# A transformer block on one core: its feed-forward part put in source order on every engine, with fixed places for small operations

## The chip, the cores and the metric

The kernel runs on one core of one Trainium2 chip. The metric is the device time of one execution in microseconds (us). Before the change it is 1748.71 us, the median of three runs (1748.16 to 1749.04). A core has five instruction queues that matter here: PE (TensorE, the matmuls), DVE (VectorE), ACT (ScalarE), POOL (GpSimd), each of which works through its instructions in the order in which they stand, and SP, which here only issues DMA transfers.

## The reference

One block on 2048 rows of width 512, batch 1:

```python
x = A_x
mod = (_silu(c) @ w_mod).reshape(c.shape[0], 6, 1, -1)
sa, ca, ga, sb, cb, gb = (mod[:, 0], mod[:, 1], mod[:, 2], mod[:, 3], mod[:, 4], mod[:, 5])
h = _layernorm(x, axis=-1) * (1 + ca) + sa
x = x + ga * _A_ref(h, A_k_cache, A_v_cache, A_wq, A_wo)
h = _layernorm(x, axis=-1) * (1 + cb) + sb
x = x + gb * _B_ref(h, B_w_gate, B_w_up, B_w_down)
return x
```

`_A_ref` is attention with 32 query heads over a cache of 512 keys; `_B_ref` is `(gelu(x @ w_gate) * (x @ w_up)) @ w_down` with a hidden width of 1792. The change touches the second half, the feed-forward part.

## The kernel before, in words

**Numbers in two halves.** Every matmul operand is held as a pair of float16 tiles, a high part (the value rounded) and a low part (the value less the high part). A product of two such pairs is three matmuls (`mm3`, L86, the matmuls' own line is L90). Making a pair is called parting: a copy to float16 on one engine, then a subtraction.

**The feed-forward part.** The hidden width is 14 slices of 128, taken two at a time: a pair of slices n. The rows are taken in two groups of 1024, so n runs from 0 to 13, and `q` from 0 to 27 (L1742): the even q is the gate set of a pair, the odd q its up set. A set is a 2 x 2 block product made with seven products instead of eight (`product`, L854; `CHAIN`, L865), in the order 1, 2, 6, 7, 5, 4, 3 (`ORDER`, L1610). Each product is 6 matmuls of 128x512. Products 1, 6, 7 and 4 add up in one PSUM bank, `fa`; 2 is in `fb`; 5 and 3 in `fc`. After products 1, 6 and 7 ScalarE copies `fa` out (`keep`, L883, line L885), because the bank goes on adding; so the next product into `fa` waits for that copy. VectorE then adds the other bank to the copy (L1270). For a gate set ScalarE applies gelu (L1276); for an up set VectorE multiplies by the gate (L1287). The four quarters of the result are called 11, 21, 22 and 12; they become ready after products 2, 4, 5 and 3.

**The projection down.** For n = 0 to 4 and 7 to 11 (`turned(n)`) it is again a seven-product block product, transposed, in two rounds of seven groups of 3 matmuls (`yt_tasks`, L1711). It needs the parted quarters 11, 21, 22 and four sums: t1 = 12 - 11, t3 = 22 - 12, t2 = 22 - t1, t4 = 21 - t2 (`sums_of`, L1300). GpSimd makes the sums (L1303) and their low parts; ScalarE makes the high parts (L1297); the low parts are L1298, on VectorE for the plain quarters. After each group VectorE adds the bank, scaled, to an accumulator `yt` (L1664, L1667). For the other four pairs it is a plain product with 8 tiles of rows, 6 matmuls each (`py`), added by VectorE (L952). These groups are slipped in, two at a time, after four of the seven products of the sets that follow (`y_next`).

**Beside it** in the first row group: the second LayerNorm of rows 1024 to 2047 (`ln_turned`, L529: load, normalize on ScalarE L539, part on ScalarE L543 and GpSimd L544, transpose by DMA), its transposed tiles scaled and shifted (`turned_out`, L553: ScalarE L558, VectorE L559, a store), and the block sums of these (`combos`, L562: GpSimd differences L574, parting on ScalarE L374 and GpSimd L378), at fixed steps (a step is one product of a set; step s is q = s // 7, product number s % 7 in the order). At the end of each row group the accumulators are turned back: a regrouping copy on GpSimd (`yt_turn`, L1678, line L1683), a DMA transpose, a copy to rows (L1701) and an addition (L1643).

**What sets the order.** `tick` runs what `put_off(k, ...)` put off by k steps (L456, L460). The attention part is written under a manual schedule for all engines (L1536): the instructions of each queue stand in the order of the source. The feed-forward part stands under a manual schedule for SP alone (L1535): DMAs are issued in source order, and a scheduler, with its own estimates of durations, arranges PE, DVE, ACT and POOL around them.

## Time and profile before

| | |
|---|---|
| median of 3 runs | 1748.71 us |
| the profiled execution's own time | 1750.29 us |
| its span (first to last instruction) | 1748.5 us |
| mean granted TensorE clock | 0.997 |
| matmuls recorded | 8020 |
| feed-forward part, from about | 1330 us on |
| DVE, ACT and POOL busy over the span | 82%, 70%, 62% |

A row of a timeline gives the start in us from the start of the span, the busy time in us, engine, line, operation, tiles written and read, shapes, a count if equal rows were merged, and in square brackets the idle time of the engine before it with what ended it. A row of groups gives the count, the busy time in us, the mean of one in ns, and the idle time ahead. A matmul's recorded time has a tail that overlaps the next one.

### The profile page before, as it was taken

To read this page: it belongs to the slowest core of one execution; us is meant where nothing else is said; L and a number is where in the kernel's file an instruction comes from. 1 tells how busy PE (TensorE), PEld (TensorE's weight loads), DVE (VectorE), ACT (ScalarE), POOL (GpSimd) and SP (SyncE) were. 2 spreads that over 40 slices of the span, in tenths; PEclk is the share of its full clock that TensorE was granted. 3 is DMA by queue.
4 is the path that set the end of the run, shared out by engine and by line. 5 is a ranking of instruction groups with operands and counts; after the bars stand their busy time and mean duration, and the time that the engine had idled before them with its cause. 6 is when DMAs were issued, how large, how long until landed. Compare 5 with 4: busy or idle time off the path is not lost.

```text
span 1748.5 us, 26169 instructions
## 1 busy us (share of the span) xinstructions
PE 1717.0 (98%) x8020; PEld 787.3 (45%) x8022; DVE 1425.4 (82%) x2454; ACT 1228.4 (70%) x2781; POOL 1085.5 (62%) x1298
## 2 busy tenths in 40 slices
PE   8999999999999999999999999999999999999998
PEld 5444444444444444444444444444444444444443
DVE  7898898888889899888887888888886787666665
ACT  5988788888879777888787777788773644333431
POOL 4889778776788884655585675654521648452435
PEclk9999999999999999999999999999999999999999
DMA  6999999999999998999999999999986753643245
GB/s 231 221 198 212 216 214 206 223 205 222 212 220 228 206 208 183 213 212 235 200 217 231 211 208 216 204 225 216 198 178 142 199 170 135 166 139 103 88 125 137
DMA packets 690637, 339.83 MB, mean 194 GB/s; under 512 B 578880, under 2 KB 601408, under 8 KB 690496
## 3 DMA queue, kind: packets, MB, share of 16 engines
q1 hardware_dynamic: 690208, 337.63, 85.6%
q8 instruction: 63, 1.03, 0.2%
q14 instruction: 78, 0.64, 0.1%
q10 hardware_dynamic: 288, 0.52, 0.1%
HBM read 135.66 MB, written 61.87 MB: 113 GB/s over the span
## 4 chain that ended last, share of the span: by engine, by line
PE 84%; DVE 5%; ACT 4%; POOL 3%; DMA 2%; issue 1%; SPq 1%; DVEq 0%; POOLq 0%; ACTq 0%
PE py L90 19%; PE ps L90 17%; PE po L90 17%; PE qa L90 8%; PE fa L90 7%; PE qc L90 4%; PE fc L90 3%; PE ya L90 2%; PE qb L90 2%; PE fb L90 2%; PE yc L90 1%; PE pq L90 1%; ACT ee L991 1%; ACT p L1003 1%; DVE nm L982 1%
## 5 line engine op out<-in xcount | busy, mean ns | idle before, releaser
L991 ACT ACTIVATE ee<-ps,nm 128x512 f32<-128x512 f32 x512 | 349.9, 683 | 194.4 <-DVE nm L982 190.1
L1008 DVE SCALAR_TENSOR_TENSOR p<-ee,rr,p 128x512 f16<-128x512 f32 x512 | 456.7, 892 | 3.9 <-ACT p L1003 3.3
L982 DVE TENSOR_REDUCE nm<-ps 128x1 f32<-128x512 f32 x512 | 350.6, 685 | 110.4 <-PE ps L90 107.5
L90 PE MATMUL ps<-k,qt 128*128 128x512 f16 x1536 | 415.6, 380 | 5.4 <-ACT ee L991 4.2
L1003 ACT ACTIVATE p<-ee,rr 128x512 f16<-128x512 f32 x512 | 364.4, 712 | 19.3 <-DVE rr L999 9.7
L90 PE MATMUL po<-pt,v 128*128 128x512 f16 x1536 | 373.1, 379 | 2.1 <-DMA pt<-p 1.2
L90 PE MATMUL py<-wo,ot 128*128 128x512 f16 x1536 | 371.6, 379 | 0.0
L90 PEld LDWEIGHTS <-w 128*128 128x128 f16 x2184 | 213.6, 98 | 269.1 <-DMA w<-kept 7.1
L90 PEld LDWEIGHTS <-v 128*128 128x128 f16 x1536 | 149.8, 98 | 184.3 <-DMA pt<-p 2.4
L90 PEld LDWEIGHTS <-ot 128*128 128x128 f16 x1536 | 150.1, 98 | 181.9 <-DVE ot L740 0.5
L90 PEld LDWEIGHTS <-qt 128*128 128x128 f16 x1536 | 145.9, 98 | 177.4 <-issue 5.4
L1303 POOL TENSOR_TENSOR fg<-fg 128x512 f32<-128x512 f32 x40 | 52.5, 1314 | 117.2 <-DVE fg L1287 116.5
L740 DVE SCALAR_TENSOR_TENSOR ot<-po,ot 128x512 f16<-128x512 f32 x128 | 87.7, 685 | 36.3 <-ACT ot L739 35.9
L1297 ACT ACTIVATE at<-fg 128x512 f16<-128x512 f32 x86 | 53.2, 626 | 89.4 <-DVE fg L1287 56.5
L991 ACT ACTIVATION_READ_ACCUMULATOR ee<-ps,nm 128x1 f32 x512 | 99.9, 195 | 0.0
L952 DVE SCALAR_TENSOR_TENSOR acc<-py,ysc,acc 128x512 f32<-128x512 f32 x128 | 94.7, 740 | 6.2 <-PE py L90 6.2
L235 POOL TENSOR_TENSOR lw<-lw,half__86 128x1 f32<-128x1 f32 x37 | 22.9, 619 | 104.5 <-DVE lw L185 104.5
L90 PE MATMUL fa<-t,w 128*128 128x512 f16 x336 | 83.0, 379 | 2.3 <-DMA w<-kept 1.4
L90 PE MATMUL qa<-t,w 128*128 128x512 f16 x348 | 84.9, 379 | 0.0
L397 POOL TENSOR_TENSOR rs<-rs,nhalf 128x1 f32<-128x1 f32 x32 | 18.7, 584 | 104.2 <-DVE rs L391 101.3
L739 ACT ACTIVATE ot<-po 128x512 f16<-128x512 f32 x128 | 73.7, 576 | 5.0 <-PE po L90 5.0
L159 POOL TENSOR_TENSOR stage<-rw,stage 128x512 f16<-128x512 f32 (+1 forms) x56 | 64.7, 1155 | 4.7
(241 smaller groups left out, 2796.5 us busy)
## 6 DMA issues: line engine op xcount, KB each, us to landing
w<-kept SPq DMA_DIRECT2D x123, 256.0 KB, 3.5
wo<-kept SPq DMA_DIRECT2D x70, 256.0 KB, 3.5
kept<-stage SPq DMA_DIRECT2D x61, 256.0 KB, 3.3
raw<-in_wo SPq DMA_DIRECT2D x56, 256.0 KB, 3.2
kept<-w SPq DMA_DIRECT2D x39, 256.0 KB, 3.4
rw<-in_wq SPq DMA_DIRECT2D x38, 256.0 KB, 3.2
hs<-hf SPq DMA_DIRECT2D x32, 256.0 KB, 3.2
pt<-p SPq DMA_TRANSPOSE x512, 3.5
```

What stands on the lines that cost most here:

```text
L90: nc.tensor.matmul(ps, a, b, start=first and n == 0, stop=last and n == 2, skip_group_check=chain)
L159: nc.gpsimd.tensor_tensor(dst[:, 1, :], src, dst[:, 0, :], op=ALU.subtract)
L235: nc.gpsimd.tensor_tensor(out, out, half_, op=ALU.pow)
L739: nc.scalar.activation(t[:, 0, :], src, AF.Copy, scale=scale)
L740: return lambda: nc.vector.scalar_tensor_tensor(t[:, 1, :], src, scale, t[:, 0, :], op0=ALU.mult, op1=ALU.subtract)
L952: nc.vector.scalar_tensor_tensor(acc[ti], st["p"], by, acc[ti], op0=ALU.mult, op1=ALU.add)
L982: nc.vector.tensor_reduce(nm, E[t]["ps"], axis=AX.X, op=ALU.max, negate=True)
L991: nc.scalar.activation(e, E[t]["ps"], AF.Exp, bias=E[t]["nm"], scale=1.0, accum_out=sm[:, t % 2:t % 2 + 1])
L1003: nc.scalar.activation(p16[:, 0, :], E[t]["e"], AF.Copy, scale=E[t]["r"])
L1008: nc.vector.scalar_tensor_tensor(p16[:, 1, :], E[t]["e"], E[t]["r"], p16[:, 0, :], op0=ALU.mult, op1=ALU.subtract)
L1297: nc.scalar.activation(t[:, 0, :], g, AF.Copy)
L1303: nc.gpsimd.tensor_tensor(g[o], g[a], g[b], op=ALU.subtract)
```

## The change

Five things change, all in the feed-forward part.

1. The whole of it is put under a manual schedule for all engines: PE, DVE, ACT and POOL now stand in source order, as SP did.
2. The subtraction that makes the low part is put off. For 11, 22 and 12 it comes two steps after the high part. For 21 it comes just before the sum that follows product 3.
3. The four sums are made one after another on GpSimd, and their parting is put off: high parts 2 steps (t1), 3 (t3, t2) and 4 (t4) later, low parts 4 (t1, t2) and 5 (t3, t4) later.
4. The LayerNorm steps get fixed places: loads 5 steps ahead instead of 4, turning 4 steps after instead of 5, other start steps; the VectorE half of `turned_out` is put off by two steps and its store by four; the block sums start 8 steps later.
5. The regrouping copy of `yt_turn` moves from GpSimd to ScalarE.

```diff
-        nc.vector.scalar_tensor_tensor(v, TURN[qb][:, :, KT + dt, :], sc, v, op0=ALU.mult, op1=ALU.add)
-        put_off(3, lambda: dma(spilled(3, qb)[:, dt, :], f))
+        put_off(2, lambda: nc.vector.scalar_tensor_tensor(v, TURN[qb][:, :, KT + dt, :], sc, v, op0=ALU.mult, op1=ALU.add))
+        put_off(4, lambda: dma(spilled(3, qb)[:, dt, :], f))
...
-        def parts(key, g, eng):
+        def high_of(key, g):
             t = A[n, key] = pair("ot", "at", NOT)
             nc.scalar.activation(t[:, 0, :], g, AF.Copy)
+
+        def low_of(key, g, eng):
+            t = A[n, key]
             eng.tensor_tensor(t[:, 1, :], g, t[:, 0, :], op=ALU.subtract)
+
+        def parts(key, g):
+            high_of(key, g)
+            if key == "21":
+                st["low"] = lambda: low_of(key, g, nc.vector)
+            else:
+                put_off(2, lambda: low_of(key, g, nc.vector))
 
         def sums_of():
             g = {k: G.pop((n, k)) for k in ("11", "12", "21", "22")}
             for o, a, b in (("11", "12", "11"), ("12", "22", "12"), ("22", "22", "11"), ("21", "21", "22")):
                 nc.gpsimd.tensor_tensor(g[o], g[a], g[b], op=ALU.subtract)
-                parts({"11": "t1", "12": "t3", "22": "t2", "21": "t4"}[o], g[o], nc.gpsimd)
+            for key, o, high, low in (("t1", "11", 2, 4), ("t3", "12", 3, 5), ("t2", "22", 3, 4), ("t4", "21", 4, 5)):
+                put_off(high, lambda key=key, o=o: high_of(key, g[o]))
+                put_off(low, lambda key=key, o=o: low_of(key, g[o], nc.gpsimd))
...
             elif k == 3:
+                if "low" in st:
+                    st["low"]()
                 add("u2", "c")
                 out_("12", st["u2"])
...
-    for i in range(2 * QT):
-        q = 7 * (2 + i // 2) + 3 * (i % 2)
+    for i, q in enumerate((16, 19, 22, 26, 30, 33, 36, 40)):
         load, norm, split, turn = ln_turned(i)
-        step(q - 4, load)
+        step(q - 5, load)
         step(q, norm)
         step(q + 1, split)
-        step(q + 5, turn)
-    for k, (qb, dt) in enumerate(((0, 0), (0, 2), (0, 1), (0, 3), (1, 0), (1, 2), (1, 1), (1, 3))):
-        step(33 + 2 * k if k < 4 else 41 + k, lambda qb=qb, dt=dt: turned_out(qb, dt))
+        step(q + 4, turn)
+    for q, (qb, dt) in zip((37, 41, 44, 47, 50, 51, 54, 55), ((0, 0), (0, 2), (0, 1), (0, 3), (1, 0), (1, 2), (1, 1), (1, 3))):
+        step(q, lambda qb=qb, dt=dt: turned_out(qb, dt))
     for p in range(2):
-        q = 53 + 14 * p
+        q = 61 + 14 * p
...
-            nc.gpsimd.tensor_copy(u, YT[g, c, qb].bitcast(U16).rearrange("p (r h) -> p h r", h=2))
+            nc.scalar.activation(u, YT[g, c, qb].bitcast(U16).rearrange("p (r h) -> p h r", h=2), AF.Copy)
...
+    ctx.enter_context(tc.manual_schedule())
     f_done = {(0, k) for k in ORDER} | {(1, 1), (1, 2), (1, 6)}
     for q in range(NQ):
```

More of the change, by code (lines that the diff above doesn't have):

```diff
@@ L1288, in result @@
                 if not turned(n):
-                    parts(key, G.pop((n, key)), nc.vector)
+                    parts(key, G.pop((n, key)))
                 elif key != "12":
-                    parts(key, g, nc.vector)
+                    parts(key, g)
                 else:
                     sums_of()
-        def parts(key, g, eng):
+        def high_of(key, g):
             t = A[n, key] = pair("ot", "at", NOT)
             nc.scalar.activation(t[:, 0, :], g, AF.Copy)
+        def low_of(key, g, eng):
+            t = A[n, key]
             eng.tensor_tensor(t[:, 1, :], g, t[:, 0, :], op=ALU.subtract)
+        def parts(key, g):
[4 more added lines that the diff above has]
+                put_off(2, lambda: low_of(key, g, nc.vector))
         def sums_of():
```

## The prediction

> **What bounds the kernel now.** I read the page's first part, then the windows of the feed-forward part, then who PE waits for there.

> ```profile
> span 1748.5 us, 26169 instructions
> ...
> PE 1717.0 (98%) x8020; PEld 787.3 (45%) x8022; DVE 1425.4 (82%) x2454; ACT 1228.4 (70%) x2781; POOL 1085.5 (62%) x1298
> ```
> ```profile
> 1330.00:1540.00 210.00, 202.53 (x934) 90.81 (x933) 145.03 (x205) 92.28 (x152) 119.05 (x112) 1.00 0.54 156
> 1540.00:1700.00 160.00, 160.00 (x743) 72.44 (x742) 107.90 (x155) 61.03 (x99) 59.12 (x48) 1.00 0.38 119
> 1700.00:1748.50 48.50, 40.17 (x176) 17.02 (x173) 27.12 (x36) 8.15 (x13) 26.12 (x21) 0.94 0.53 139
> ```
> ```profile
> PE fa L90 <- DMA w<-kept: 5.3, 3, 2.2
> PE yc L90 <- ACT at L1297: 2.6, 2, 2.0
> PE py L90 <- ACT at L1297: 1.6, 2, 0.8
> PE fc L90 <- DVE fg L1270: 1.0, 1, 1.0
> PE fa L90 <- ACT fg L885: 0.6, 1, 0.6
> PE py L90 <- DVE at L1298: 0.4, 1, 0.4
> PE fa L90 <- ACT fu L885: 0.2, 1, 0.2
> ```

> PE is the bound: 98% of the span, and 160.00 of 160 us in the middle stretch. (The columns are PE, PEld, DVE, ACT, POOL, clock, DMA share, GB/s.) The change adds and removes no matmul, so it can only act through what PE waits for, in 418.5 of 1748.5 us. Those waits are the seven rows (from 1290 us on): 11.7 us in 11 waits. Two things come on top.

> ```profile
> 1484.27 0.59 PE L90 MATMUL yc<-at,wo 128*128 128x512 f16 x2 [1.95 <-ACT at L1297]
> 1484.69 1.46 PE L90 MATMUL fb<-b,w 128*128 128x512 f16 x6
> ...
> 1711.72 1.46 PE L90 MATMUL fc<-b,w 128*128 128x512 f16 x6
> 1715.43 2.46 PE L90 MATMUL fa<-b,w 128*128 128x512 f16 x6 [2.24 <-DMA w<-kept]
> 1717.68 2.20 PE L90 MATMUL fb<-b,w 128*128 128x512 f16 x6
> ```

> Six matmuls normally show 1.46 us; the next start comes 1.30 us after (0.216 each), so a tail of 0.16 us overlaps. Each wait loses that overlap too: 11 x 0.16 = 1.8 us. And after the wait of 2.24 us the next twelve matmuls ran at half rate: 2.46 + 2.20 - 2 x 1.46 = 1.74 us. After the wait of 1.95 us none did. So **15.2 us are lost now** (11.7 + 1.8 + 1.7), the most that the change can win.

> **What it removes.** The order of the built instructions shows that it does what it says: on PE, DVE, ACT and POOL the feed-forward part stands in source order.

> ```profile
> L1683 POOL COPY yu<-yt 128x1024 uint16<-128x1024 uint16 x16 | 17.2, 1098 | 29.0 <-DVE yt L1664 26.5 <-DMA yv<-yu 2.5
> ```
> ```profile
> SPq L1688 <- POOL yu L1683: 29.6, 4, 12.4
> ```

> SP, already in source order, stood 29.6 us behind transposes whose input POOL had not yet copied; weight loads are queued behind them, and PE's 5.3 us of DMA waits follow. With the copy on ACT at its source place I let these waits go, with their clock loss, and what is late next is in the sum below. The two `py` rows are at the very end: there the new order puts two tiles of pair 12 (12 matmuls, 2.6 us) between the last product 3 and the first tile of pair 13, and the low parts it needs are made in that time. I let all 15.2 us go.

> **What it adds: one new chain a pair.** In the new order ACT makes the high parts of t3 and t2 *before* it copies `fa` after product 6 of the next gate set (both put off by 3 steps). Product 7 waits for that copy, and t2 is GpSimd's third subtraction. In the scheduler's order nothing forced that. The durations:

> ```profile
> L1303 POOL TENSOR_TENSOR fg<-fg 128x512 f32<-128x512 f32 x40 | 52.5, 1314 | 117.2 <-DVE fg L1287 116.5
> L1298 POOL TENSOR_TENSOR at<-fg,at 128x512 f16<-128x512 f32 x40 | 48.7, 1226 | 1.1 <-ACT at L1297 1.1
> L1297 ACT ACTIVATE at<-fg 128x512 f16<-128x512 f32 x85 | 52.5, 626 | 87.5 <-DVE fg L1287 54.7 <-POOL fg L1303 32.7
> L574 POOL TENSOR_TENSOR cb<-cb 128x512 f32<-128x512 f32 x8 | 11.5, 1436 | 0.1
> L378 POOL TENSOR_TENSOR t<-cb,t 128x512 f16<-128x512 f32 x8 | 10.1, 1268 | 0.0
> L559 DVE SCALAR_TENSOR_TENSOR hf<-xt,cols,hf 128x512 f32<-128x512 f16 x8 | 9.1, 1181 | 1.8 <-ACT hf L558 1.8
> ```
> ```profile
> 1585.78 0.63 ACT L1297 ACTIVATE at<-fg 128x512 f16<-128x512 f32 x1
> 1586.44 0.69 DVE L1298 TENSOR_TENSOR at<-fg,at 128x512 f16<-128x512 f32 x1 [0.69 <-ACT at L1297]
> 1587.05 0.74 DVE L1287 SCALAR_TENSOR_TENSOR fg<-fg,gsc,fa 128x512 f32<-128x512 f32 x1
> ...
> 1589.02 0.68 DVE L1298 TENSOR_TENSOR at<-fg,at 128x512 f16<-128x512 f32 x1
> 1589.62 0.68 DVE L1270 TENSOR_TENSOR u<-u,fc 128x512 f32<-128x512 f32 x1
> 1590.22 0.75 DVE L1664 SCALAR_TENSOR_TENSOR yt<-yb,dyc,yt 128x512 f32<-128x512 f32 x1
> 1590.88 0.68 DVE L1270 TENSOR_TENSOR fg<-fg,fb 128x512 f32<-128x512 f32 x1
> 1591.48 0.75 DVE L1287 SCALAR_TENSOR_TENSOR fg<-fg,gsc,u 128x512 f32<-128x512 f32 x1
> ...
> 1592.37 2.62 POOL L1303 TENSOR_TENSOR fg<-fg 128x512 f32<-128x512 f32 x2 [15.70 <-DVE fg L1287]
> ...
> 1597.90 0.58 ACT L885 ACTIVATE fg<-fa 128x512 f32<-128x512 f32 x1
> 1598.61 0.60 ACT L885 ACTIVATE u<-fa 128x512 f32<-128x512 f32 x1
> ```

> Queued on DVE, an addition or a low part takes 0.60 us to the next start, a scaled addition or multiplication 0.66 (0.72 if it needs the one just before), and its result is there after 0.75; POOL starts 0.14 after that, two subtractions take 2.62 us, a third 1.27 (0.04 of overlap); a full ACT starts a part each 0.54. Handing over between other engines costs 0.03 to 0.05.

> Take t = 0 where DVE can start the sum after product 5 of an up set. Its queue then is: that sum 0; multiply 22 at 0.72; multiply 21 at 1.37; low part of 22 at 2.18 (its high part on ACT runs 1.51 to 2.14); two `yt` additions 2.78, 3.44; low part of 21 at 4.10; the sum after product 3 at 4.70; multiply 12 at 5.42, done 6.17. POOL subtracts from 6.31, the third is done at 10.16; ACT makes t2's high part from 10.18, copies `fa` 10.72 to 11.32; PE can go at 11.37. PE's own way from t = 0 is 48 matmuls, less the tail and the hand-over: 48 x 0.216 - 0.20 = 10.17. **PE waits 1.2 us.** Product 3's sum alone was ready 0.8 us before its place in the queue.

> Ten pairs have such sums. By the order of each:
> - n = 8 to 11: 4 x 1.2 = 4.8; n = 1 the same, 1.2.
> - n = 0: only 36 matmuls lie between (no groups of an earlier pair), and no `yt` additions: chain 10.1, own way 7.6, 2.5 us.
> - n = 2: one VectorE half of `turned_out` (1.18) stands ahead of the gate's sum, so gelu, which is ahead of t2 on ACT, is a little late: 1.4.
> - n = 3: two such halves stand there; sum after product 2 at 9.8, gelu 10.5, t3, t2 and the copy behind it to 12.7: 2.5.
> - n = 4: 1.2, and POOL's order there puts two block-sum differences and two low parts (2 x 1.44 + 2 x 1.27 = 5.4) between the four subtractions (done 11.4) and the low parts of t1 and t2 (2 x 1.2): t2 is whole at 19.2, PE wants it at 68 x 0.216 + 1.2 = 15.9: 3.3 more.
> - n = 7: beside a plain pair, one addition fewer: 0.6.
> - The 16 regrouping copies on ACT: no row has ACT doing 1024 numbers. It lies between one 512 part (0.63) and two (1.25); I take 1.05, near two, since the size is doubled. Most have cover: ACT was idle 87.5 us before its parts alone. In the gate set of pair 6 three of them and three other parts stand ahead of the copy of `fa`: about 1.0 us; with 0.63 each nothing, with 1.25 some 1.6.

> Together 4.8 + 1.2 + 2.5 + 1.4 + 2.5 + 4.5 + 0.6 + 1.0 = **18.5 us**. Two of these, at n = 0 and n = 4, are longer than the 2.24 us after which the clock halved; 2 x 1.74 = 3.5. The place of n = 3 is near that limit, and I leave it out. The put-off low parts cost PE nothing: 11, 21 and 22 are needed 4 to 15 us after. LayerNorm loads go out a step earlier, stores later; their readers are over 10 us away.

> **The sum:** 18.5 + 3.5 - 15.2 = +6.8 us on the profiled execution's 1750.29 us, 1757.1. That execution is 1.6 us above the median, so I put the median at 1748.71 + 6.8 = **1755.5**.

> [...]

> **The rivals.**
> - *No half rate.* The new waits come, but spread so that no stretch of PE is idle enough; 1.95 us cost nothing in this trace. Then 18.5 - 15.2 = +3.3: 1752.0, just inside no change. [...] For it: mean clock 0.997, only one such stretch.
> - *Faster.* The chain has 1.2 us less than I count, because the waits feed back on each other: any stop of PE inside the 48 matmuls gives DVE, POOL and ACT that time. Point from which it decides: chain 10.2 us or less. Then n = 1, 2, 8 to 11 and 7 cost 0.2 at most, n = 0 and 3 cost 1.3 each, n = 4 3.3, pair 6 1.0, clock 1.7: 8.8 - 15.2 = -6.4: 1742.3. For it: in the middle stretch the same operations made PE wait for nothing.
> - *Weights still late.* If ACT's copies come late in their turn, SP stays behind transposes as now: 5.3 + 0.5 + 1.7 stay: 1763. Against: ACT has more free time there than POOL.
> - That the order doesn't change is excluded by the built program.

> **Chances.** Forecast 0.50; no half rate 0.20; faster 0.18; weights late 0.12. A measurement tells about 0.2% (3.5 us) from no change: slower 0.62, same 0.20, faster 0.18. The forecast's own range is 1752.5 to 1760. The range to hold 8 in 10 takes in no half rate and reaches half into the two outer cases: 1743 to 1763. It covers copies of 0.63 and 1.25 us.

> **What would show it.** Right: in the profile after, PE's largest row is `fa` waiting for ACT L885, about 1 us each, ten times, 27 us apart; the waits for weights are gone; a wait for POOL's low part once, near the tenth set. Wrong: no such row, or rows for weights; a wait of over 2.3 us without half rate refutes the clock term, a POOL subtraction well under 1.2 us the chain.

## The result, and the profile after

The changed kernel takes **1762.76 us** (median of 4 runs, 1761.17 to 1763.47), the kernel before on the same chip 1748.43 us (4 runs, 1747.65 to 1749.04): ratio 1.0081, 95% interval 1.0063 to 1.0098. It is 14.3 us slower. The forecast was 6.8 us slower, 1755.5.

The page's first part, after:

```profile
span 1761.0 us, 26246 instructions
...
PE 1718.3 (98%) x8020; PEld 788.1 (45%) x8022; DVE 1415.7 (80%) x2454; ACT 1242.6 (71%) x2797; POOL 1063.9 (60%) x1282
```

PE's busy time is the same as before to 1.3 us (1717.0), its span is 12.5 us longer: PE waits more. In the middle stretch, where PE was busy for 160.00 of 160 us, it is now busy for 154.38 (columns as in the prediction's table):

```profile
1540.00:1700.00 160.00, 154.38 (x710) 69.33 (x709) 100.86 (x145) 58.46 (x95) 57.31 (x47) 1.00 0.36 112
```

Whom PE waits for from 1290 us on:

```profile
PE fa L90 <- ACT fg L885: 14.7, 14, 3.4
PE ya L90 <- DVE yt L1677: 6.5, 10, 0.7
PE fa L90 <- ACT u L885: 1.0, 1, 1.0
```

The waits for weights and the two at the very end for parts are gone. In their place stand 14 waits for ScalarE's copy of `fa`, and ten, which the forecast did not have, of a group of the projection down for an addition to `yt`. In this kernel's line numbers L885 is the copy, L1297 a high part, L1301 a low part, L1313 a subtraction of the sums, L1677 an addition to `yt`, L1270 a sum of two banks, L1287 a multiplication.

Below, **lost** is what matmul starts are apart beyond 0.216 us, summed from 1330 us on; it takes in the lost overlap and half-rate stretches. Before the change it is 15.3 us, after it 29.5. The difference, 14.2, agrees with the 14.3 us between the medians. The two profiled spans differ by less, 12.5 us, because the profiled execution of the kernel before lost some 2 us more ahead of 1330 us (18.2 against 16.0). By place, beside the forecast:

| place | forecast | lost: `ya` + product 7 + product 4 |
|---|---|---|
| n = 0 | 2.5 | 2.72 (product 7) |
| n = 1 | 1.2 | 0.82 + 0.70 + 0.48 = 2.00 |
| n = 2 | 1.4 | 0.82 + 1.11 + 0.92 = 2.85 |
| n = 3 | 2.5 | 0.82 + 2.07 = 2.89 |
| n = 4 | 4.5 | 0.82 + 1.24 + 3.55 = 5.61 |
| pairs 5 and 6 | 1.0 | 0.82 + 0.33 = 1.15 |
| n = 7 | 0.6 | 0.73 |
| n = 8 to 11 | 4.8 | 4 x (0.82 + 0.77) = 6.4 |
| end | 0 | 0.82 + 1.14 = 1.96 |
| half rate | 3.5 | 3.3 in two stretches |
| sum | 22.0 | 29.6 |

The largest of these places, n = 4, where ScalarE's copy waits for a GpSimd low part and PE for the copy:

```profile
1493.10 0.60 ACT L885 ACTIVATE fg<-fa 128x512 f32<-128x512 f32 x1 [5.02 <-POOL at L1301]
...
1493.75 1.55 PE L90 MATMUL fa<-t,x 128*128 128x512 f16 x6 [3.39 <-ACT fg L885]
```

Pair 9 in the timeline, the rows of its chain:

```profile
1624.55 1.46 PE L90 MATMUL fa<-t,x 128*128 128x512 f16 x6
1624.82 0.69 DVE L1270 TENSOR_TENSOR u<-u,fc 128x512 f32<-128x512 f32 x1 [1.76 <-PE fc L90]
...
1626.99 0.69 DVE L1301 TENSOR_TENSOR at<-fg,at 128x512 f16<-128x512 f32 x1
...
1628.45 0.75 DVE L1677 SCALAR_TENSOR_TENSOR yt<-ya,dyc,yt 128x512 f32<-128x512 f32 x1
...
1629.12 0.68 DVE L1301 TENSOR_TENSOR at<-fg,at 128x512 f16<-128x512 f32 x1
1629.25 0.81 PE L90 MATMUL ya<-at,wo 128*128 128x512 f16 x3 [0.65 <-DVE yt L1677]
...
1631.33 5.33 POOL L1313 TENSOR_TENSOR fg<-fg 128x512 f32<-128x512 f32 x4 [19.00 <-DVE fg L1287]
...
1634.75 1.21 ACT L1297 ACTIVATE at<-fg 128x512 f16<-128x512 f32 x2
...
1635.87 0.58 ACT L885 ACTIVATE fg<-fa 128x512 f32<-128x512 f32 x1
...
1636.50 0.81 PE L90 MATMUL fa<-t,w 128*128 128x512 f16 x3 [0.61 <-ACT fg L885]
```

The forecast chain is there, step by step: from the sum after product 5 to product 7 it takes 1636.50 - 1624.82 = 11.68 us, against 11.37 forecast and 10.17 of PE's own. PE loses this time in two portions: 0.82 at a group of three matmuls, whose bank VectorE empties late because a low part stands ahead of the addition, and 0.77 at product 7.

### The profile page after: what moved, and what is told of

Same layout as the page of the kernel before. It is cut to its first block, busy times and chain, and to the rows that moved or that the text cites. A ratio compares the mean times of both kernels' runs of the same rounds, so it can differ in the third digit from the quotient of the medians.

```text
span 1761.0 us, 26246 instructions
## 1 busy us (share of the span) xinstructions
PE 1718.3 (98%) x8020; PEld 788.1 (45%) x8022; DVE 1415.7 (80%) x2454; ACT 1242.6 (71%) x2797; POOL 1063.9 (60%) x1282
## 4 chain that ended last, share of the span: by engine, by line
PE 83%; DVE 7%; ACT 5%; POOL 2%; issue 2%; DMA 1%; DVEq 0%; SPq 0%; POOLq 0%; ACTq 0%
PE py L90 19%; PE ps L90 17%; PE po L90 17%; PE qa L90 8%; PE fa L90 6%; PE qc L90 4%; PE fc L90 3%; PE ya L90 2%; PE qb L90 2%; PE fb L90 2%; ACT ee L991 1%; PE yc L90 1%; ACT p L1003 1%; PE pq L90 1%; DVE nm L982 1%
## 5 line engine op out<-in xcount | busy, mean ns | idle before, releaser
L90 PE MATMUL ps<-k,qt 128*128 128x512 f16 x1536 | 414.9, 379 | 5.6 <-ACT ee L991 4.5
L90 PE MATMUL po<-pt,v 128*128 128x512 f16 x1536 | 372.9, 379 | 1.8 <-DMA pt<-p 1.8
L90 PE MATMUL py<-wo,ot 128*128 128x512 f16 x1536 | 371.5, 379 | 0.1
L90 PEld LDWEIGHTS <-w 128*128 128x128 f16 x2184 | 213.8, 98 | 272.6 <-issue 16.9
L90 PEld LDWEIGHTS <-v 128*128 128x128 f16 x1536 | 149.9, 98 | 184.1 <-DMA pt<-p 2.0
L90 PEld LDWEIGHTS <-ot 128*128 128x128 f16 x1536 | 150.2, 98 | 181.7 <-DVE ot L740 0.5
L90 PEld LDWEIGHTS <-qt 128*128 128x128 f16 x1536 | 145.9, 98 | 177.0 <-issue 4.5
L1313 POOL TENSOR_TENSOR fg<-fg 128x512 f32<-128x512 f32 x40 | 51.9, 1298 | 151.5 <-DVE fg L1287 149.1
L1297 ACT ACTIVATE at<-fg 128x512 f16<-128x512 f32 x86 | 53.3, 626 | 79.2 <-DVE fg L1287 74.3
L90 PE MATMUL fa<-t,w 128*128 128x512 f16 x336 | 81.6, 379 | 11.2 <-ACT fg L885 10.2
L90 PE MATMUL qa<-t,w 128*128 128x512 f16 x348 | 84.9, 379 | 0.0
L90 PE MATMUL ya<-at,wo 128*128 128x512 f16 x240 | 63.9, 382 | 6.5 <-DVE yt L1677 6.5
```

Of the source, the lines that this page charges most:

```text
L90: nc.tensor.matmul(ps, a, b, start=first and n == 0, stop=last and n == 2, skip_group_check=chain)
L1297: nc.scalar.activation(t[:, 0, :], g, AF.Copy)
L1313: nc.gpsimd.tensor_tensor(g[o], g[a], g[b], op=ALU.subtract)
```

## Experiments

All kernels are edits of the changed kernel unless said otherwise. Each time stands beside the kernel before run on the same chip (medians 1748.1 to 1749.1). In the diffs `...` stands for lines left out, and a line that begins inside a statement is the changed piece of it. All waits and losses are read in the one profiled execution of each kernel, from 1290 or 1330 us on; where that execution lies off the median, the text says so.

### The low part of 22 behind the additions to yt

```diff
-            if key == "21":
-                st["low"] = lambda: low_of(key, g, nc.vector)
+            if key in ("21", "22"):
+                st["low" + key] = lambda: low_of(key, g, nc.vector)
...
+                    st["low22"]()
+                    st["low21"]()
                 add("u2", "c")
```

> The changed kernel with one thing altered: VectorE's low part of 22 stands behind the two additions to yt, still ahead of the low part of 21 and of the sum after product 3, so that GpSimd's start stays as it is in VectorE's queue and no low part runs beside GpSimd. Theory A (one chain a pair): the ten waits of 0.82 us for yt go, but in the eight pairs in which GpSimd's subtractions follow, product 7 then waits that much longer for the copy of fa (0.77 becomes 1.5 to 1.6 us in pairs 8 to 11); only the two places without subtractions behind them win, 1.6 us: 1762.8 - 1.6 = 1761 us. Rival B (the wait for yt is a loss of its own beside the chain): 1762.8 - 8.2 = 1754.6 us.

Measured: 1763.16 us, ratio 1.0083 (1.0069 to 1.0096), the changed kernel's time. PE's waits:

```profile
PE fa L90 <- ACT fg L885: 20.1, 14, 3.9
...
PE ya L90 <- DVE yt L1678: 0.6, 2, 0.4
```

`ya`'s 6.5 us went to 0.6, and the wait for the copy grew from 14.7 to 20.1; in pairs 8 to 11 product 7 loses 1.38 instead of 0.77, and 0.09 is left at `ya`, 1.47 together against 1.59. Theory A holds in the main: in a pair with sums the wait for `yt` is a part of the chain, taken early, and moving it wins next to nothing. The 1.6 us that theory A expected from the two places without sums does not show in the time; in this execution other losses stand against it, among them a wait of 1.0 us for weights.

### Low parts behind the last multiplication

The same two low parts were put further back, right behind the multiplication of 12.

```diff
                 nc.vector.scalar_tensor_tensor(g, g, col("gsc", n % NP), src, op0=ALU.mult, op1=ALU.mult)
+                if key == "12":
+                    st["low21"]()
+                    st["low22"]()
```

> The changed kernel with one thing altered: in the up sets VectorE's low parts of 21 and 22 stand right behind the multiplication of 12 (and ahead of GpSimd's subtractions in the program, which overwrite their input), instead of ahead of the additions to yt and of the sum after product 3. Theory A: the ten waits of 0.82 us for an addition to yt go (8.2 us). The sum after product 3 starts as soon as the product is there, 0.8 us earlier in the chain, so GpSimd starts about 0.8 us earlier against PE's own way, and the wait of product 7 for the copy of fa shrinks from 0.77 to about 0.5 us: 1762.8 - 8.2 - 10 x 0.3 = 1751.6 us. Rival B (what is won at ya is lost again at the copy, since the chain through GpSimd alone sets the pace): ya goes, the wait for the copy grows to about 1.6 us, 1762 us.

Measured: 1768.89 us, ratio 1.0112 (1.0097 to 1.0127): slower than the change. `ya` is free, and product 7 loses 1.63 in pairs 8 to 11: the number of rival B, and more than the shorter queue should leave. Pair 9, VectorE and GpSimd:

```profile
1633.92 2.36 DVE L1304 TENSOR_TENSOR at<-fg,at 128x512 f16<-128x512 f32 x2
...
1634.14 5.96 POOL L1316 TENSOR_TENSOR fg<-fg 128x512 f32<-128x512 f32 x4 [18.48 <-DVE fg L1287]
```

Two low parts take 2.36 us instead of 1.3, and the four subtractions beside them 5.96 instead of 5.33. VectorE is so late for the next gate's sum that gelu, which stands ahead of the copy of `fa`, is late too. The slowdown is taken up below. The profiled execution (1766.12 us, clock 0.998) is the shortest of the four; the other three, 1768.2 to 1769.7, have clocks of 0.995 and 0.996, so part of the 6 us over the change is probably half rate that this trace does not show.

An earlier form put the low parts off by two and four steps, alone and together with the edits of the next two sections.

```diff
-                put_off(2, lambda: low_of(key, g, nc.vector))
+            put_off(4 if key == "22" else 2, lambda: low_of(key, g, nc.vector))
```

There they are made from what GpSimd's subtractions have left in the tiles of 21 and 22, so both kernels compute other low parts than the reference needs, and VectorE has to wait for GpSimd:

> The changed kernel with one thing altered: VectorE's low parts of 21 and 22 in the up sets stand behind the multiplication of 12 and the additions to yt, instead of ahead of them (low part of 21 put off by two steps, of 22 by four). Theory A (the queues in source order): in the changed kernel PE waits 0.82 us ten times for an addition to yt (ya, 8.2 us together) because a low part of 0.60 us and an earlier addition stand ahead of it; this wait goes. The sum after product 3 also comes some 0.8 to 1.2 us earlier, and with it GpSimd's four subtractions; since PE now also arrives 0.82 us earlier, the wait of product 7 for the copy of fa shrinks only a little, from 0.77 to about 0.5 us. 1762.8 - 8.2 - 10 x 0.3 = 1751.6 us. Rival B (one chain: what is won at ya is lost again at the copy of fa, since the chain through GpSimd sets the pair's pace): ya goes, but the wait for the copy grows to about 1.6 us; 1762 us.

> The changed kernel with the three alterations together: low parts of 21 and 22 behind the multiplication of 12, high parts of t3 and t2 behind the copy of fa, block operations five steps later in pair 4. Theory A (four separate queue places account for the whole loss): of the 29.5 us that PE loses from 1330 us on in the changed kernel, 8.2 (ya), 12 (copy of fa), 4.5 (product 4) and 3.3 (half rate) go; 1762.8 - 28 = 1734.8 us, which is 13.6 us less than the kernel before. What is left: the two VectorE halves in pair 3 and about 1 us at the end. Rival B (the waits feed on one chain, and PE meets the next late result a little further on): a sum of the single gains is not reached; about 1748 us, no better than the kernel before.

Measured: 1834.99 and 1831.48 us, ratios 1.0493 (1.0477 to 1.0508) and 1.0473 (1.0457 to 1.0488). They answer neither question; they show what a wait of VectorE for GpSimd costs: in the first, PE waits 24.4 us in ten places for a low part and 47.9 us in twelve for the copy of `fa`, with half rate besides: the granted clock is 0.977 over the span and 0.93 from 1540 to 1700 us.

### High parts behind the copy of fa

```diff
-("t3", "12", 3, 5), ("t2", "22", 3, 4)
+("t3", "12", 4, 5), ("t2", "22", 4, 4)
```

> The changed kernel with one thing altered: ScalarE's high parts of t3 and t2 are put off by four steps instead of three, so they stand behind the copy of fa after product 6, not ahead of it. Theory A: the waits of product 7 for that copy (13.1 us in 12 places, 0.77 us in each of pairs 8 to 11) go nearly all, and with the 2.72 us at the first of them also the 1.7 us of half rate that follow it; the low parts of t2 come in time (18 matmuls, 3.9 us, lie between product 7 and the first group that reads t2). The waits for yt and the 3.55 us of pair 4 stay. 1762.8 - 12.5 - 1.7 = 1748.6 us. Rival B (the wait only moves on): the groups of the next pair then wait for t2's low part about as long as product 7 waited for the copy; about 1759 us.

Measured: 1757.44 us, ratio 1.0049 (1.0033 to 1.0066): 5 us of the expected 14. In pairs 8 to 11 product 7 waits no more, and 0.14 is left at product 4. But in pairs 0, 1, 2 and 4 product 4 now loses 1.45, 1.19, 2.04 and 4.58 (7.1 with the half rate behind it): the *next* copy of `fa` has no buffer, because its tile still holds t1's sum until GpSimd has made t1's low part. Pair 2, ScalarE and GpSimd:

```profile
1430.32 1.61 POOL L544 TENSOR_TENSOR xh<-xs,xh 128x512 f16<-128x512 f32 x1
1431.89 3.38 POOL L1301 TENSOR_TENSOR at<-fg,at 128x512 f16<-128x512 f32 x3
...
1433.07 0.60 ACT L885 ACTIVATE fg<-fa 128x512 f32<-128x512 f32 x1 [2.04 <-POOL at L1301]
```

A LayerNorm parting (L544) stands ahead of that low part. (The profiled execution took 1762.44 us, the other three 1757.0 to 1757.6. It lost 20.9 us ahead of 1330 us, against 16.0 in the change's; from 1330 us on it lost 24.1 against 29.5, which is the 5 us of the medians.) So neither theory is right as it stood: the wait does move on, but to a buffer, not to t2's low part.

### Block operations later in pair 4

```diff
-                step(q + 2 * off, fn)
+                step(q + 2 * off + (5 if p == 0 and off > 3 else 0), fn)
```

> The changed kernel with one thing altered: of the first half of GpSimd's block sums in the feed-forward part, the differences and low parts that stand between the subtractions and the low parts of pair 4 are put five steps later. Theory A: ScalarE's copy of fa after product 7 in pair 4 stood idle 5.02 us for GpSimd's low part of t1, because the copy goes into the buffer that this low part still reads, and four block operations (4.8 us) stand ahead of it. With these gone the wait of 3.55 us at product 4 goes, and with it the half rate of 1.63 us behind it; all other waits stay: 1762.8 - 5.2 = 1757.6 us. Rival B (GpSimd is late there by the subtractions alone, or the displaced block operations are late for another pair): 1761 us or more, with a wait at the same place or one new in pair 5 or 6.

Measured: 1769.33 us, ratio 1.0117 (1.0102 to 1.0132). The wait of 3.55 us in pair 4 is gone, as theory A has it, and a larger one is there 17 us later:

```profile
1510.90 1.46 PE L90 MATMUL fa<-t,w 128*128 128x512 f16 x3 [8.27 <-DMA w<-kept]
```

SP stood 10.57 us at the loads for the second half of the block sums, which wait for buffers that the first half now frees later; the weight load behind them was late. Rival B's second form.

### Which of the edits does what: order, copies, put-off parts

The kernel before with the fixed order alone; the change without the fixed order; the change with the regrouping copy back on GpSimd. The edits, in this order:

```diff
+    ctx.enter_context(tc.manual_schedule())
     f_done = {(0, k) for k in ORDER} | {(1, 1), (1, 2), (1, 6)}
...
-    ctx.enter_context(tc.manual_schedule())
     f_done = {(0, k) for k in ORDER} | {(1, 1), (1, 2), (1, 6)}
...
-            nc.scalar.activation(u, YT[g, c, qb].bitcast(U16).rearrange("p (r h) -> p h r", h=2), AF.Copy)
+            nc.gpsimd.tensor_copy(u, YT[g, c, qb].bitcast(U16).rearrange("p (r h) -> p h r", h=2))
```

> The kernel before with one line added: the fixed source order on PE, VectorE, ScalarE and GpSimd for the feed-forward part; no copy, low part, LayerNorm step or block sum is moved. Theory A (a fixed order makes each engine wait where the program puts a dependent instruction right behind its source): GpSimd makes each low part directly behind its subtraction and waits for ScalarE's high part in between, four times (1.31 + 0.63 + 1.14 each, 12 us instead of 5.3 before the copy of fa can go); product 7 waits some 6 us in ten pairs, each followed by a half-rate stretch of about 1.7 us: 1748 + 10 x 7.7 = about 1825 us. Rival B (the order alone costs no more than with the edits, so the put-off parts do nothing): about 1765 us.

> The changed kernel without its fixed source order on the engines: the scheduler places the feed-forward part again, as in the kernel before, and the other edits (copies on ScalarE, low parts put off, LayerNorm and block places) stay. Theory A (the fixed order makes the loss, the copies on ScalarE win back the waits for weights): the waits for yt and for the copy of fa are gone as before the change, the 5.3 us of waits for weights and their 1.7 us of half rate are gone too; about 1743 us. Rival B (the moved places of the other edits cost by themselves, with the scheduler following them): 1755 us or more. Rival C (the scheduler's order brings back the waits for weights whatever engine copies): 1748 us.

> The changed kernel with one thing undone: the 16 regrouping copies are on GpSimd again (1.10 us each in the kernel before), at the same places of the fixed order. Theory A (the copy's place on ScalarE is what took the waits for weights away): SP again stands behind transposes whose input is not copied yet, weight loads are queued behind them, and waits for weights of about 5 us come back, with a half-rate stretch: 1762.8 + 6 = 1769 us. Rival B (the fixed order takes them away whatever engine copies, since GpSimd then makes each copy in its turn): no wait for weights, 1762 to 1764 us.

Measured: 1905.85 us (ratio 1.0898, 1.0879 to 1.0917), 1751.01 us (1.0014, 1.0004 to 1.0024) and 1765.27 us (1.0092, 1.0077 to 1.0107). The order alone costs 157 us, even more than expected: beside 90.9 us at the copy there are 42.0 at `yt`. GpSimd there, in one pair:

```profile
1689.61 1.27 POOL L1303 TENSOR_TENSOR fg<-fg 128x512 f32<-128x512 f32 x1 [30.62 <-PE yc L90]
1691.62 1.15 POOL L1298 TENSOR_TENSOR at<-fg,at 128x512 f16<-128x512 f32 x1 [0.74 <-ACT at L1297]
1692.73 1.26 POOL L1303 TENSOR_TENSOR fg<-fg 128x512 f32<-128x512 f32 x1
```

One subtraction each 3.1 us instead of 1.3. The other edits together win back 143 of these 157 us. The rows point to the put-off parts, but no run has these alone. Without the fixed order the same edits cost 2 us (1751.01 against 1749.08), so some 12 of the change's 14.3 us come with the fixed order. And PE's waits with the scheduler and the copies on ScalarE:

```profile
PE fa L90 <- DMA w<-kept: 5.6, 3, 3.8
PE fc L90 <- DVE fg L1270: 2.8, 1, 2.8
```

The waits for weights are all there (5.3 us before). They are absent in the order alone, and in the fixed order with the copy on GpSimd, whose rows are the changed kernel's plus a longer `yt` row (8.9 us). So the fixed order removes them, not the copy's engine; 1765.27 against 1762.76 is too near to say more of the engine.

### All queue places, then the places of other work

The low parts stand behind the multiplication of 12 as above. New in the first kernel:

```diff
-            for o, a, b in (("11", "12", "11"), ("12", "22", "12"), ("22", "22", "11"), ("21", "21", "22")):
+            for o, a, b in (("11", "12", "11"), ("12", "22", "12"), ("22", "22", "11")):
...
-            for key, o, high, low in (("t1", "11", 2, 4), ("t3", "12", 3, 5), ("t2", "22", 3, 4), ("t4", "21", 4, 5)):
+            for key, o, high, low in (("t1", "11", 2, 2), ("t2", "22", 4, 4), ("t3", "12", 4, 5), ("t4", "21", 4, 5)):
...
+                if key == "t1":
+                    put_off(2, lambda: minus("21", "21", "22"))
```

and in the second, besides:

```diff
-    for i, q in enumerate((16, 19, 22, 26, 30, 33, 36, 40)):
+    for i, q in enumerate((17, 20, 22, 25, 31, 33, 36, 39)):
...
-zip((37, 41, 44, 47, 50, 51, 54, 55),
+zip((33, 35, 42, 44, 48, 49, 50, 58),
...
+    LOADS, MOVED = iter((75, 75, 76, 77)), {69: 73, 71: 74, 73: 75, 75: 76}
-        q = 61 + 14 * p
+        q = (61, 77)[p]
-            step(q - 2, load)
+            step(next(LOADS) if p else q - 2, load)
-                step(q + 2 * off, fn)
+                step(MOVED.get(q + 2 * off, q + 2 * off) if p == 0 else q + 2 * off, fn)
```

> As the kernel with the low parts behind the multiplication of 12, and besides: ScalarE's high parts of t2 and t3 stand behind the copy of fa after product 6, and GpSimd makes the low part of t1 ahead of its fourth subtraction (the copy of fa after product 7 goes into the buffer that this low part reads, and waited 0.14 to 2 us for it when only the high parts were moved). LayerNorm's places and the block sums stay as in the change. Theory A: in pairs 8 to 11 nothing of the 1.6 us a pair is left; pair 4 keeps about 4 us behind the block sums and perhaps a half-rate stretch, pairs 0, 2 and 3 about 1 us each, the end 1.2 us; of 29.5 us about 11 are left: 1762.8 - 18.5 = 1744 us, under the kernel before. Rival B (one more late result behind each that goes, t2's low part next): about 0.8 us a pair is left, 1752 us.

> As the kernel with all queue places altered, and besides the places of other work: the block operations of pair 4 that stood between GpSimd's subtractions and low parts go three to four steps later (their loads for the second half two steps later, one by one), GpSimd's LayerNorm partings leave the last step of an up set, and VectorE's LayerNorm halves leave the steps around the sum after product 2 in pairs 2 and 3. Theory A: of the 29.5 us lost in the changed kernel only the 1.2 us at the end and some 2 us are left: 1762.8 - 26.3 = 1736.5 us, 12 us under the kernel before. Rival B (the displaced work is late elsewhere, loads for the block sums ahead of weights on SP above all): a new wait for a transfer in pairs 4 to 6, 1742 us or more.

Measured: 1758.89 us (1.0059, 1.0044 to 1.0074) and 1749.78 us (1.0008, 0.9999 to 1.0018), 15 and 13 us above theory A. The places of other work were worth 9 us (7.5 expected), but in each of pairs 3, 4 and 8 to 11 product 7 still lost 0.59 and product 4 0.24: gelu stood ahead of the copy and waited for VectorE, held up by its slow low parts. That is 5.0 of the 15.4 us lost there; the rest lies mostly in pairs 0 to 2 and 5 to 7 and at the end. Two remedies, gelu behind the copy and t1's low part ahead of the third subtraction; and the same with the low parts ahead of the sum after product 3, where GpSimd is idle:

```diff
-                    step()
+                    put_off(2, step) if key == "11" else step()
...
                 if key == "t1":
+                    put_off(2, lambda: minus("22", "22", "11"))
                     put_off(2, lambda: minus("21", "21", "22"))
```

> As the kernel with all places altered (1749.8 us, 15.2 us lost from 1330 us on, of these 0.59 at the copy of fa after product 6 and 0.24 at the copy after product 7 in each of pairs 3, 4 and 8 to 11), with two places more: the gelu of the gate set's first output is put off behind the copy of fa after product 6 (the copy stood behind it, and it behind VectorE's low parts, which took 2.36 us for two while GpSimd subtracts, 0.69 us each elsewhere), and GpSimd makes t1's low part ahead of its third subtraction. Theory A: both waits go in all ten pairs; left are about 1 us in pairs 0, 6 and at the end each, and 0.3 to 0.5 in a few others, some 5.5 us: 1749.8 - 9.7 = 1740 us, which beats the kernel before by 0.5%. Rival B (VectorE's queue, longer by the contended low parts, makes the next addition late): 0.4 us or more is left in each pair, 1746 us.

> As the kernel with the gelu put off and t1's low part ahead of the third subtraction, but VectorE's low parts of 21 and 22 stand ahead of the sum after product 3 (behind the additions to yt), so that GpSimd is not yet at its subtractions. Theory A (VectorE's low parts and GpSimd's subtractions, both with two inputs in SBUF, hold each other up): a low part takes 0.6 to 0.7 us again and GpSimd's subtractions 1.27 instead of 1.42 us each. The chain starts 1.05 us later by the queue and wins 0.6 us on GpSimd; it has some 2 us of slack by then, so the time is that of the other kernel to within 2 us. Rival B: the low parts take 1.0 us or more here too, since it is not GpSimd that slows them.

Measured: 1756.66 us (1.0048, 1.0036 to 1.006) and 1765.52 us (1.0096, 1.0079 to 1.0113). Product 7 is free; product 4 now loses 1.44 a pair (1.75 in the second). Pair 9 of the first, ScalarE:

```profile
1630.94 1.15 ACT L1300 ACTIVATE at<-fg 128x512 f16<-128x512 f32 x2 [1.34 <-POOL fg L1316]
1632.29 0.63 ACT L1300 ACTIVATE at<-fg 128x512 f16<-128x512 f32 x1 [0.20 <-POOL fg L1316]
1632.83 0.71 ACT L1276 ACTIVATE fg<-fg,finv 128x512 f32<-128x512 f32 x1
1633.44 0.57 ACT L885 ACTIVATE fg<-fa 128x512 f32<-128x512 f32 x1
```

The copy after product 7 stands behind t4's high part, whose subtraction had just become later, and behind gelu. Both remedies were right and the queue behind them was not looked at. In the second kernel the start of the subtractions, 1 us later, comes on top. That kernel was expected within 2 us of the first and is 9 us slower: the 2 us of slack that the expectation counted on are not there. Its six executions run from 1761.12 us (clock 1.000) to the profiled one, 1771.31 (0.995, with 6.4 us lost to four half-rate stretches), so how many of its waits cost clock changes from one execution to the next. For the slow low parts it decides: over pairs 8 to 11 of the kernel of "Low parts behind the last multiplication", where they stand beside the subtractions, and of this second kernel, where they do not (GpSimd's rows first):

```profile
L1316 POOL TENSOR_TENSOR fg<-fg 128x512 f32<-128x512 f32 x16 | 22.9, 1432 | 74.3 <-DVE fg L1287 73.4
...
L1304 DVE TENSOR_TENSOR at<-fg,at 128x512 f16<-128x512 f32 x12 | 12.2, 1040 | 0.0
```
```profile
L1313 POOL TENSOR_TENSOR fg<-fg 128x512 f32<-128x512 f32 x16 | 20.4, 1274 | 78.1 <-DVE fg L1287 77.4
...
L1301 DVE TENSOR_TENSOR at<-fg,at 128x512 f16<-128x512 f32 x12 | 7.9, 682 | 0.0
```

### The last two places

```diff
-("t3", "12", 4, 5), ("t4", "21", 4, 5)
+("t3", "12", 5, 5), ("t4", "21", 5, 5)
...
-                    put_off(2, step) if key == "11" else step()
+                    waits_.insert(0, [2, step]) if key == "11" else step()
```

> As the kernel with the gelu put off and t1's low part ahead of the third subtraction (1756.7 us), with two places more: ScalarE's high parts of t3 and t4 stand behind the copy of fa after product 7, and the gelu ahead of t2's high part. In that kernel the copy after product 7 stood behind t4's high part, which waits for GpSimd's fourth subtraction (1.15 us later than before by the moved low part), and behind the gelu; PE lost 1.44 us there in each of ten pairs, 2.80 in pair 0 and 2.26 in pair 2. Theory A: these are the last late results in the pair, and nothing new is late: of 22.5 us lost some 6 are left (the end 0.85, additions to yt in pairs 1, 2, 4 and 5 about 2.5, pair 0 about 1), 1756.7 - 16.5 = 1740 us, 0.5% under the kernel before. Rival B (one late result more: the low parts of t3 or t4 come late for the groups that read them): 0.5 us or more a pair is left, 1745 us or more.

Measured: **1739.66 us** (5 runs), ratio 0.9951 (0.9937 to 0.9965). All of PE's waits from 1290 us on:

```profile
PE ya L90 <- DVE yt L1685: 1.6, 4, 0.7
PE fa L90 <- ACT u L885: 0.7, 1, 0.7
PE fa L90 <- ACT fg L885: 0.7, 1, 0.7
```

5.1 us are lost, none to half rate (granted clock 1.000), and PE is busy for 160 of 160 us in the middle stretch again. Theory A's 1740 holds. This version is 8.9 us faster than the kernel before and 23 us faster than the change: the fixed order, with other places, beats both. What the scheduler would make of these places was not run.

## Why the prediction was right in kind and wrong in size

- **Direction and mechanism held.** The largest row is `fa` waiting for ACT L885, once a pair, 28.8 us apart; removing the high parts from ahead of the copy freed product 7 in pairs 8 to 11. All 15.2 us of old loss went, as assumed, though for another reason: "With the copy on ACT at its source place I let these waits go" names the copy, and the runs show the place.
- **The step that failed** is the tally of the new waits: "Together ... 18.5 us", where 26.3 were lost, 24.3 up to pair 11 and 2.0 at the end. So the time came out at 1762.8, above the forecast's own range of 1752.5 to 1760. The three mis-sized parts:
  - "PE waits 1.2 us" was 1.6 in pairs 8 to 11 (1.6 us in all). The chain was 0.31 us longer: VectorE's second addition waited for its group of matmuls (0.19), GpSimd and ScalarE took 0.1 more. And t = 0 comes 0.27 us after PE's next matmul (1624.82 against 1624.55), not 0.20 as the -0.20 in PE's own way has it.
  - The *second* copy of `fa` was not followed. Its buffer holds t1's sum, and so it waits for t1's low part: 0.48 and 0.92 at n = 1 and 2. At n = 4 the forecast had the right delay, block sums ahead of the low parts (3.3 forecast, 3.55 lost), but put it on t2's low part. With `ya`'s 0.82 and the rest these three pairs lost 3.4 us more than forecast, n = 3 another 0.4.
  - "The put-off low parts cost PE nothing" is wrong as it stands: low parts ahead of the additions to `yt` cost 0.82 in ten places. In eight this is the chain's own time, taken earlier; in pairs 5 and 12, which have no sums, no chain follows and it is a loss. With 1.14 at the end, where I had put nothing, that gives the 2.0 us of the table's end, and pairs 5 and 6 are as forecast by luck: the copies cost 0.33 instead of 1.0 there, and `ya` 0.82 instead of nothing.
- **Half rate**: two stretches of 1.66 and 1.63 us after the waits at n = 0 and n = 4, forecast 2 x 1.74. The number held, the rule behind it did not, and that is luck. The prediction went by the length of a wait, 2.24 us, and named its own sign of being wrong: "a wait of over 2.3 us without half rate refutes the clock term". In the kernel with 22's low part moved, the waits at n = 0 and n = 4 lost 2.73 and 4.02 us, against 2.72 and 3.55 in the change, and neither cost clock; what the traces show of this is in the last section. The rival without half rate is refuted for the change. So is the rival of late weights: that its number, 1763, is the measured one is chance, since no wait for weights is left. The faster rival, in which the waits feed back on each other until little is left, was wrong for this kernel: the chain is over 10.2 us. What the feedback does is decide *where* in the pair the loss shows.
- The ScalarE copy of 1024 numbers, taken at 1.05 us, took 1.05. VectorE's halves at L559, taken at 1.18 each, took 0.74 ahead of the gate's sum in pair 2, and 0.75 and 1.79 in pair 3: 2.54 together against 2.36.

## What to carry to other kernels

When queues are fixed, follow each engine's queue past the first late result: here every place that was mended uncovered the next instruction in line (high parts, then a buffer, then gelu, then t4's high part), and only the kernel with all of them mended came out under the kernel before, 23 us under the change. A wait that goes may only have been a portion of a chain taken early, so cost the chain, not the row. Buffers count as queue places: the reader that frees a tile belongs to the chain of whoever writes it next.

## What the runs showed of the hardware

**VectorE and GpSimd hold each other up.** A subtraction with both inputs in SBUF took VectorE 0.68 us where GpSimd was not subtracting (the kernel with the low parts ahead of the sum after product 3) and 1.2 on average for the two beside GpSimd's subtractions (low parts behind the last multiplication), and these took 1.43 instead of 1.27; the four additions to `yt` beside them in pair 9, with one input in PSUM, took 0.73 to 0.75. One by one, in pair 9 of the latter kernel, above: VectorE's first low part, already running when GpSimd starts, takes 0.68 us and the second 1.76; it ends 0.55 us after GpSimd's first subtraction. That first subtraction and the second take 1.58 and 1.60 us, the other two 1.27.

**The half-rate stretches lie on a grid, and the wait's length alone did not decide.** In the trace of the change the two stretches with a granted clock of 0.50 begin at 1368.68 and 1494.98 us and last 3.413 us each; their starts are 126.29 us apart, 37 times that length. In the kernel before, such a stretch of 3.413 us begins at 1715.76 us and the next at 1746.48, 30.72 us or 9 times that length later. Windows along the grid of each trace, of the change (columns: PE busy, granted clock, DMA share, GB/s), and of the kernel with 22's low part moved (columns as in the prediction's table; PE busy is the first):

```profile
1365.30:1368.70 3.40, 1.32 (x7) 1.00 0.00 0
1368.70:1372.10 3.40, 3.40 (x10) 0.50 0.00 0
```
```profile
1489.20:1492.60 3.40, 1.41 (x7) 0.55 (x6) 0.00 (x0) 0.00 (x0) 3.40 (x4) 1.00 0.02 8
1492.60:1496.00 3.40, 1.53 (x8) 0.70 (x8) 0.69 (x1) 2.18 (x4) 3.40 (x5) 1.00 0.26 69
1496.00:1499.40 3.40, 3.40 (x17) 1.54 (x16) 2.26 (x4) 2.23 (x5) 3.40 (x5) 1.00 0.29 80
```
